# Turning q and k on TensorE instead of VectorE for the first batch's strided heads and the second batch's local heads

## The chip, the cores and the metric

The kernel runs on one core of a Trainium2 chip. The metric is the device time in microseconds of one execution, as the median of three runs. Where an engine is named: PE is TensorE, DVE is VectorE, ACT is ScalarE, POOL is GpSimd, SP is SyncE (here it only issues DMAs).

## The reference

Four batches of eight heads, 576 positions, head size 64. The first four heads of a batch attend locally, the other four with a stride; the attention's output goes through two MLPs.

```
scores = scale * np.matmul(q, k.transpose(0, 1, 3, 2))
mask_local = (rel >= 0) & (rel < stride)                      # heads 0 to 3, stride 32
mask_strided = (rel >= 0) & (pos[None, :] % stride == pos[:, None] % stride)   # heads 4 to 7
attn = softmax(where(mask, scores, -1e9));  x = attn @ v      # x becomes 2304 x 512
y = (x @ w_a) * (x @ w_b) @ w_out                             # d_ff 1536
h = y @ w_in;  out = (h * sigmoid(h)) @ w_out2                # d_ff 2048
```

## The kernel before, in words

The order of the work is written out by hand: each engine runs its instructions in the order in which the Python code issues them, and waits where a value or a buffer is not ready.

**Start-up.** The attention of batch 0 is cut into nine units: five of local heads (128 queries each) and four of strided heads. A loop over stages `s` from -1 to 16 runs one step of each unit per stage, in the order of the letters in `ORDER`: within a stage come V (`values`), then Q (the strided q and k of batch 0 are turned, by the table `TQ`, in stages 2, 3 and 4), then S (`scores`, L414 and L417), T (`turn`, L500) and K. K is `keep_warm` (L773): matmuls of constants whose result nobody reads, so many per stage as `WARM1` says. The DMAs of the start-up are issued in the order of `LOADS[-2]`: small letters on SP's queue, capitals on ACT's; `t` is one step of the loads of batch 0's strided q and k, `u` one of batch 1's local q and k, `s` and `v` are values, `w` weights as 64-bit words.

The local q and k of batch 0 are turned on TensorE in pairs of positions (`turn_pair`, L296, evacuated at L307 and L309). All other q and k are loaded by `load_qk` (L264): eight DMAs, each of 32-element pieces (128 bytes) into 32 partitions, laid out so that four VectorE stream transposes (`transpose_qk`, L275, 128x576 each) make `qT` and `kT`.

**Blocks.** After the start-up the MLP of the first tokens runs in blocks `p`: kinds a, b (up, L683, 12 matmuls of 512 columns) and o (down, L1345, 12). The first four up blocks have half of their matmuls in the start-up (`PART`, four times 6); the last two of these halves come after the last unit of batch 0, and the other halves are blocks 0 to 3, 6 matmuls each. Block 4 is the first o block; it needs the gated product of block 1 (L1331 on VectorE, then a split: L693 on ScalarE, L694 on VectorE). The attention of batches 1 to 3 is woven into these blocks by `plan_attention`: `PLAN[1]` gives the blocks at which the nine units of batch 1 are prepared, a unit's scores stand two blocks later, its turn five and its values six. At the head of a block come the functions planned under "load", "tensor" and "turned", then the block's matmuls, then the planned VectorE and ScalarE work.

**Buffers.** In batch 0 `att_tile` hands out seven PSUM banks in turn (later four); for batches 1 to 3 it hands out two, so the third request waits for the readers of the first. The tiles `qld` and `kld` have one buffer each.

Around block 0 VectorE and ScalarE also finish two weight tiles that were begun early (`merge_w`, L642 to L655; their splits L675 and L676).

Of the kernel before, what the change touches and what calls it, by code (L numbers as in the profile page):

```python
# [9 lines left out]
F32 = mybir.dt.float32  # L10
# [8 lines left out]
P = 128  # L19
# [14 lines left out]

PREP = {-1: (0, 1, 2, 3, 4), 3: (5, 6), 5: (7,), 7: (8,)}
PAIR = {-1: 0, 0: 1, 2: 2}
TQ = {2: (0,), 3: (1,), 4: (2, 3)}

LOADS = {
    -2: (  # L40
        "q0 Q1 i M1 K2 S1 w0 V1 k0 k1 s1 t4 t5 v0 M7 r8 s1 s1 s1 w2 s2 s1 S1 w1 s1 s1 s1 w4 "
        "w3 s4 Q2 u2 u5 u2"
    ),
    -1: "b",
    8: "w5 w6",
# [48 lines left out]


PLAN = {
# [3 lines left out]
}  # L100
# [11 lines left out]
def attention_gated_mlp_silu_mlp(  # L112
# [15 lines left out]
    nc = tc.nc  # L128
    B, H, S, D = q.shape
# [32 lines left out]
    lpool = att_ctx.enter_context(tc.tile_pool(name="lpool", bufs=1, side="right"))  # L162
    qpool = att_ctx.enter_context(tc.tile_pool(name="qpool", bufs=2, side="right"))
    apool = att_ctx.enter_context(tc.tile_pool(name="apool", bufs=3, side="right"))

    ident = cpool.tile([P, P], F32, name="ident")
# [11 lines left out]
    def acc_tile(i):  # L178
        return accp.tile([P, 512], F32, tag=f"acc{i}", name=f"acc{i}")

    def ring_tile():
        return ringp.tile([P, 512], F32, tag="ring", name="ring")

    att_turn = [0]
    feed = [nc.sync]

    def att_tile(wide):
        n = att_turn[0]
        att_turn[0] += 1
        if wide:  # L190
            n %= wide
            if n < 2:
                return ring_tile()
            if n >= 4:
                return acc_tile(n - 4)
        return attp.tile([P, 512], F32, tag="att", name="att")
# [36 lines left out]
    class Batch:  # L233
# [38 lines left out]
        def transpose_qk(self, ty, one=None):  # L272
            for i in range(4) if one is None else (one,):
                t, o, c = self.loaded[i // 2], self.T[ty][i // 2], i % 2
                nc.vector.transpose(out=o[:, c], in_=t[:, c].rearrange("p j i -> p (j i)"))  # L275

        def load_pair(self, m, i):

            if not self.T:
                self.T[0] = [qpool.tile([P, 2, S], F32, tag=nm, name=nm) for nm in ("qT", "kT")]  # L280
                self.pairs = {}
            p0, n = PAIRS[m]
            self.pairs[m, i] = t = rpool.tile([P, 4, 2 * D], F32, tag="raw", name="pair")
            feed[0].dma_start(
                out=t[:n],
                in_=(q, k)[i][self.b, 0:4, 2 * p0:2 * (p0 + n), :].rearrange("h (p s) d -> p h (s d)", s=2),
            )
# [392 lines left out]
    def up(ps, w, x, T, chunks=range(CC)):  # L680
        for c in chunks:
            for wi, xi in PASSES:
                nc.tensor.matmul(  # L683
                    ps[:, :T],
                    lhsT=w[:, wi, c * P:(c + 1) * P],
                    rhs=x[:, xi, c, :T],
                    start=(c == 0 and wi == 0 and xi == 0),
                    stop=(c == CC - 1 and wi == 1),
                )
# [12 lines left out]
    def plan_attention(batch, s0, first, end):  # L702

        add = lambda at, place, f, *a: plan.setdefault((at, place), []).append((f, a))

        def spread(loads, n, s0, s1):
            for m in range(n):
                add(s0 + m * (s1 - s0) // n, "load", next, loads, None)

        turn1 = first[NL - 1] + 2  # L710
        for one in range(4):
            add(s0 + one // 2, "prepare", batch.transpose_qk, 0, one)
            add(turn1 - 4 + one, "prepare", batch.transpose_qk, 1, one)
        spread(batch.load_qk(1), 9, s0 + 2, turn1 - 7)
        spread(batch.load_vs(), 4 * TAKE + 5, s0 + 4 * (batch.b > 1), first[NL] + 3)
        for u, s in enumerate(first):
            add(s, "prepare", batch.prepare, u)
            add(s + 2, "tensor", batch.scores, u)
            add(s + 2, "mask", batch.mask, u)
            add(s + 2, "mask", batch.largest, u)  # L720
            add(s + 2, "softmax", batch.softmax, u)
            add(s + 2, "normalise", batch.guard, u)
            add(s + 2, "normalise", batch.normalise, u)
            add(s + 5, "tensor", batch.turn, u)
            add(s + 5, "turned", batch.turned, u)
            add(s + 6, "tensor", batch.values, u)
            add(s + 6, "store", batch.store, u)
        after = Batch(batch.b + 1, False)
        if after.b < B:
            spread(after.load_qk(0), 9, turn1 + 2, end)  # L730
            spread(after.load_vl(), 10, first[NL] + 7, end)
        return after
# [30 lines left out]
    with tc.manual_schedule():  # L763
# [6 lines left out]
        def keep_warm(n):  # L770

            for _ in range(n):
                nc.tensor.matmul(idle, lhsT=still, rhs=nc.const_aps.tensor(1.0, [P, 512], BF16), start=True, stop=True)  # L773

        batch = Batch(0, 7)
        nu = len(batch.units)
        every = lambda loads: [None for _ in loads]
        after = Batch(1, False)
        qs0, vs0, q1 = batch.load_qk(1), batch.load_vs(), after.load_qk(0)
        vl0 = batch.load_vl()  # L780

        masks = [epool.tile(list(t.shape), F32, tag="e", name="mask") for t in (mask_loc, mask_str)]
# [32 lines left out]
        for s in range(-1, max(nu + LV, max(PART), max(CONV) + 1) + 1):  # L815
            def stage(f, d):
                if 0 <= s - d < nu:
                    f(s - d)

            if s >= TAIL:  # L820
                batch.wide = 4
            now, last = CONV.get(s), CONV.get(s - 1)
            for step in ORDER:
                if step == "P" and s in PAIR:
                    for i in range(2):
                        batch.turn_pair(PAIR[s], i)
                        batch.turned_pair(PAIR[s], i)
                elif step in "SVTXLGNOU":
                    f, d = {
                        "S": (batch.scores, 0), "L": (batch.largest, 0), "X": (batch.softmax, 1),  # L830
                        "G": (batch.guard, 1), "N": (batch.normalise, 1), "T": (batch.turn, LT),
                        "U": (batch.turned, LT), "V": (batch.values, LV), "O": (batch.store, LV),
                    }[step]
                    stage(f, d)
                elif step == "K":
                    keep_warm(WARM1.get(s, 0))
                elif step == "A" and s in PART:
                    i = PART[s]
                    partial[i] = acc_tile(i)
                    up(partial[i], split[i], x_tile(0), G, (0, 1))  # L840
                elif step == "Q":
                    for i in TQ.get(s, ()):
                        batch.transpose_qk(1, i)
                elif step == "R":
                    for u in PREP.get(s, ()):
                        batch.prepare(u)
                elif step in "012" and now is not None:
                    merge_w(now, int(step), True)
                elif step == "B" and now is not None:
                    rebase_w(now, True)  # L850
                elif step == "Y" and last is not None and last < EARLY:
                    keep_w(last)
                    split_w(last)
                elif step == "W":
                    startup_loads(LOADS.get(s, ""))
        batch = after
# [356 lines left out]
        for m, key in enumerate(in_order):  # L1213
            t = ready[key]
            if m >= 4:
                t = max(t, held[in_order[m - 4]][1])
# [5 lines left out]
        for m, key in enumerate(in_order):  # L1222
            t = used[key][0] - LEAD_SPLIT
            t = max(t, used[in_order[m - 5]][1] if m >= 5 else (m - 5) * BLOCK)
# [34 lines left out]
        for key in in_order:  # L1259
            t = splits[key]  # L1260
# [3 lines left out]
            elif key[0] == "B":  # L1264
                n, c = key[1:]
                kind, j = ("ab"[c], n[1]) if n[0] == "o" else ("i", n[1] + c)
                needs((kind, j), (n, c, 0), t)
            elif key[0] == "B22":
                for c in range(2):
                    n = key[1]  # L1270
                    kind, j = ("ab"[c], n[1] + H1) if n[0] == "o" else ("i", n[1] + c + H2)
                    needs((kind, j), (n, c, 1), t)
            elif key[0] == "T12":
                n, c = key[1:]
# [21 lines left out]
        for m, key in enumerate(in_order):  # L1296
            lo, _, piece = need[key]
            t = lo - LEAD_RAW
            t = max(t, need[in_order[m - 10]][1] + 0.01 if m >= 10 else (m - 10) * BLOCK)
# [3 lines left out]
        p = 0  # L1303
        ys = {}
        for ph, g in PHASES:
# [7 lines left out]
            for kind, j in half[ph]:  # L1313
                if batch.b < B and p == PLAN[batch.b][0]:
                    batch = plan_attention(batch, *PLAN[batch.b])
                work = block(p)
                w = next(work)
                if kind in "abi":
                    rest = range(CC)
                    if p in partial:  # L1320
                        ps, rest = partial[p], (2, 3)
                    else:
                        ps = ring_tile()
# [9 lines left out]
                    else:  # L1333
# [4 lines left out]
                            out=g2, in0=th, scalar=1.0, in1=ps, op0=ALU.add, op1=ALU.mult  # L1338
                        )
                        acts[j] = split_act(g2, T)  # L1340
                elif kind == "o":
                    h = acts.pop(j)
# [9 lines left out]
                    if j == N1 - 1:  # L1352
                        ys[g] = y = xpool.tile([P, 2, CC, G], F32R, tag="x%d" % HOMES["y"][g], name="y")
                        for d in range(CC):
                            nc.scalar.copy(out=y[:, 0, d], in_=accs[d])
                            nc.vector.tensor_tensor(
                                out=y[:, 1, d], in0=accs[d], in1=y[:, 0, d].bitcast(F32), op=ALU.subtract
# [3 lines left out]
                else:  # L1361
                    h = acts.pop(j)
# [14 lines left out]
            for t in range(T // P):  # L1377
                pool, tag = ((epool, "e"), (epool, "e"), (tpool, "a"), (tpool, "h32"))[t]
# [48 lines left out]
```

## Time and profile before

| | us |
|---|---|
| median of 3 runs (956.31 to 957.92) | 957.8 |
| the profiled execution | 954.39 |
| its span, first to last instruction | 952.6 |
| TensorE busy in the span | 928.5 (97%) |
| VectorE busy | 663.9 (70%) |
| ScalarE busy | 542.6 (57%) |
| mean granted TensorE clock | 0.988 |

Times in the trace are microseconds from the first instruction of the span. A busy share is an average over stages with different limits. The ends of matmuls are modelled, so that a TensorE shown as busy can still be slower than its peak. The granted clock is a share of 2.4 GHz; in this trace it is 1.00 or 0.50 (1.2 GHz).

### The profile page before, as it was taken

The numbers are of one execution on the slowest core, as the hardware profiler recorded it, in microseconds if no ns is written. First come the engines' busy times: TensorE is split into PE (matmuls) and PEld (weight loads), VectorE is DVE, ScalarE is ACT, GpSimd is POOL, SyncE is SP. The second block draws the span as 40 slices with busy tenths as digits, with TensorE's granted clock in tenths as the row PEclk, the third lists the DMA queues.
The fourth block names the chain that finished last, engine by engine and source line by source line (L and its number), as shares of the span: only waits on it lengthen the run. The fifth ranks groups of instructions, "written<-read, shape, count | busy, mean of one in ns | idle before, by whom it ended". The sixth has DMA issues, their size and how long they took to land.

```text
span 952.6 us, 15861 instructions
## 1 busy us (share of the span) xinstructions
PE 928.5 (97%) x5626; PEld 749.6 (79%) x5626; DVE 663.9 (70%) x1248; ACT 542.6 (57%) x1274; POOL 80.4 (8%) x138
## 2 busy tenths in 40 slices
PE   9999999999999899999999999999999989999998
PEld 5767777787777677778888888888998768888897
DVE  4588888866767766666777666765587666765475
ACT  3558788566667665465544444345565555554364
POOL 2232222111111110100000000000000000000000
PEclk9799999999999999999999999999999999999999
DMA  9999899898698994322332222223464121234371
GB/s 165 198 271 269 248 254 271 248 294 240 224 267 208 264 223 133 105 86 89 100 105 83 67 67 67 57 83 112 126 185 125 44 67 56 78 107 148 108 212 47
DMA packets 163647, 145.29 MB, mean 153 GB/s; under 512 B 96800, under 2 KB 119904, under 8 KB 163568
## 3 DMA queue, kind: packets, MB, share of 16 engines
q1 hardware_dynamic: 154758, 121.81, 48.1%
q0 software_dynamic: 6720, 21.63, 6.8%
q10 hardware_dynamic: 2090, 0.84, 0.5%
q8 instruction: 44, 0.72, 0.3%
q14 instruction: 35, 0.29, 0.1%
HBM read 121.70 MB, written 22.54 MB: 151 GB/s over the span
## 4 chain that ended last, share of the span: by engine, by line
PE 75%; DVE 11%; ACT 8%; issue 3%; DMA 2%; SPq 0%; DVEq 0%; POOL 0%; ACTq 0%; POOLq 0%
PE ring L683 17%; PE ring L958 10%; PE att L958 8%; PE acc L1019 8%; PE acc L1365 7%; PE acc L1145 4%; PE att L1019 4%; PE ring L1019 4%; PE acc L1345 4%; PE acc L683 3%; ACT prs L466 2%; DVE w L676 2%; DVE raw L650 2%; PE att L540 1%; ACT raw L647 1%
## 5 line engine op out<-in xcount | busy, mean ns | idle before, releaser
L683 PE MATMUL ring<-x,w 128*128 128x512 f32 (+1 forms) x816 | 165.5, 356 | 1.5 <-DVE w L676 1.5
L683 PEld LDWEIGHTS ring<-x,w 128*128 128x128 f32 x816 | 132.4, 189 | 23.4 <-DVE w L676 2.0
L1241 DVE TENSOR_TENSOR w<-raw,w 128x512 fp32r<-128x512 f32 (+1 forms) x164 | 106.3, 656 | 30.3 <-ACT w L1240 27.5
L1240 ACT CAST w<-raw 128x512 fp32r<-128x512 f32 (+1 forms) x164 | 95.8, 593 | 18.6 <-PE att L1019 11.0
L676 DVE TENSOR_TENSOR w<-raw,w 128x512 fp32r<-128x512 f32 x136 | 92.8, 686 | 8.6 <-ACT w L675 7.9
L683 PE MATMUL ring<-y,w 128*128 128x512 f32 x384 | 96.1, 400 | 2.2 <-DVE g L1337 0.8
L1365 PE MATMUL acc<-w,h 128*128 128x512 f32 x384 | 93.9, 394 | 0.0
L683 PEld LDWEIGHTS ring<-y,w 128*128 128x128 f32 x384 | 71.9, 191 | 18.8 <-DVE w L676 1.1
L675 ACT CAST w<-raw 128x512 fp32r<-128x512 f32 x136 | 82.8, 619 | 4.0 <-DVE raw L655 3.9
L1365 PEld LDWEIGHTS acc<-w,h 128*128 128x128 f32 x384 | 70.9, 188 | 15.4
L693 ACT CAST h<-h 128x512 fp32r<-128x512 f32 (+1 forms) x48 | 27.3, 568 | 95.1 <-DVE h L1331 48.1
L1345 PE MATMUL acc<-h,w 128*128 128x512 f32 x288 | 70.8, 395 | 0.0
L958 PE MATMUL ring<-operands,w 128*128 128x512 f32 x240 | 61.4, 398 | 2.4 <-ACT w L1240 2.0
L694 DVE TENSOR_TENSOR h<-g,h 128x512 fp32r<-128x512 f32 (+1 forms) x64 | 39.9, 624 | 33.4 <-ACT h L693 33.2
L1345 PEld LDWEIGHTS acc<-h,w 128*128 128x128 f32 x288 | 53.0, 188 | 11.5
L693 ACT CAST h<-g 128x512 fp32r<-128x512 f32 (+1 forms) x64 | 36.3, 568 | 44.8 <-DVE g L1337 30.4
L958 PE MATMUL att<-operands,w 128*128 128x512 f32 x240 | 60.2, 395 | 0.0
L958 PE MATMUL ring<-x,w 128*128 128x512 f32 x240 | 59.2, 391 | 1.0 <-ACT u L969 1.0
L466 ACT ACTIVATE prs<-sm,nm 128x54 f32<-128x54 f32 (+1 forms) x120 | 39.8, 336 | 30.5 <-DVE nm L452 30.4
L958 PEld LDWEIGHTS ring<-operands,w 128*128 128x128 f32 x240 | 44.7, 188 | 14.8 <-ACT w L1240 2.7
L650 DVE SCALAR_TENSOR_TENSOR raw<-words,raw 128x512 int32<-128x512 int32 x68 | 47.6, 699 | 9.5 <-ACT raw L647 8.9
L958 PEld LDWEIGHTS ring<-x,w 128*128 128x128 f32 x240 | 44.9, 188 | 11.1 <-ACT u L969 1.4
(200 smaller groups left out, 1577.1 us busy)
## 6 DMA issues: line engine op xcount, KB each, us to landing
raw<-keptp SPq DMA_DIRECT2D x80, 256.0 KB
raw<-kepti SPq DMA_DIRECT2D x64, 256.0 KB
words<-in_moe_w_out_dram SPq DMA_DIRECT2D x28, 512.0 KB
raw<-kepto SPq DMA_DIRECT2D x48, 256.0 KB
raw<-kepta SPq DMA_DIRECT2D x36, 256.0 KB
raw<-keptb SPq DMA_DIRECT2D x36, 256.0 KB
words<-in_moe_w_in_dram SPq DMA_DIRECT2D x16, 512.0 KB
words<-in_moe_w_a_dram SPq DMA_DIRECT2D x12, 512.0 KB
```

The source lines that it names most:

```text
L466: nc.scalar.activation(out=place[s], in_=src[:, s], func=AF.Exp, bias=st["nm"][:, s:s + 1], scale=1.0, accum_out=su[:, s:s + 1],)
L650: nc.vector.scalar_tensor_tensor(out=z, in0=high, scalar=SIGN, in1=z, op0=ALU.bitwise_and, op1=ALU.bitwise_or)
L675: nc.scalar.copy(out=o[:, 0], in_=t)
L676: nc.vector.tensor_tensor(out=o[:, 1], in0=t, in1=o[:, 0].bitcast(F32), op=ALU.subtract)
L683: nc.tensor.matmul(ps[:, :T], lhsT=w[:, wi, c * P:(c + 1) * P], rhs=x[:, xi, c, :T], start=(c == 0 and wi == 0 and xi == 0), stop=(c == CC ...
L693: nc.scalar.copy(out=o[:, 0, :T], in_=t32[:, :T])
L958: nc.tensor.matmul(self.acc[acc], lhsT=w[:, wi, (2 * part + c) * P:(2 * part + c + 1) * P], rhs=x[:, xi, c], start=(begin and c == 0 and m ...
L1019: nc.tensor.matmul(accs[d], lhsT=lhsT, rhs=rhs, start=(first and wi == 0 and xi == 0), stop=(last and wi == 1))
L1240: nc.scalar.copy(out=o[:, 0, cols], in_=t)
L1241: nc.vector.tensor_tensor(out=o[:, 1, cols], in0=t, in1=o[:, 0, cols].bitcast(F32), op=ALU.subtract)
L1345: nc.tensor.matmul(accs[d], lhsT=w[:, wi, d * P:(d + 1) * P], rhs=h[:, xi], start=(j == 0 and wi == 0 and xi == 0), stop=(j == N1 - 1 and ...
L1365: nc.tensor.matmul(accs[t][:, :DM], lhsT=h[:, xi, t * P:(t + 1) * P], rhs=w[:, wi, :], start=(j == 0 and wi == 0 and xi == 0), stop=(j == ...
```

## The change

For batch 0's strided heads and batch 1's local heads, `load_rows` takes the place of `load_qk`: twelve DMAs in place of eight, of whole rows of 64 elements (256 bytes). Positions 0 to 511 go by head, one DMA each for q and k (128 partitions, four positions each, 512 rows); the last 64 positions go by two heads (64 partitions, 128 rows). `turn_rows` transposes them on TensorE into a PSUM bank: i = 0 to 3 stands for q or k and one pair of heads (four transposes of 128x128), i = 4 and 5 for the last 64 positions of q and of k (two transposes of 64x128). `turned_rows` copies the bank to `qT` or `kT`: i = 0 and 3 on ScalarE, the others on VectorE. In the start-up, i = 0 stands in stage 2, 1 and 4 in stage 3, and 2, 3 and 5 in stage 4. For batch 1, i = 0 and 2 stand at the head of block 0, 4 and 5 at block 1, 1 and 3 at block 2, with two PSUM banks to share; the first scores move from block 3 to block 4, and all nine units of batch 1 one block later. Batch 1's strided q and k, and all of batches 2 and 3, are loaded and turned as before.

```
-TQ = {2: (0,), 3: (1,), 4: (2, 3)}
+TQ = {2: (0,), 3: (1, 4), 4: (2, 3, 5)}
+TOKENS = 4
+ROWS_A = (0, 3)
-        "q0 Q1 i M1 K2 S1 w0 V1 k0 k1 s1 t4 t5 v0 M7 r8 s1 s1 s1 w2 s2 s1 S1 w1 s1 s1 s1 w4 "
-        "w3 s4 Q2 u2 u5 u2"
+        "q0 Q1 i M1 K2 S1 w0 V1 k0 k1 s1 t6 t7 v0 M7 r8 s1 s1 s1 w2 s2 s1 S1 w1 s1 s1 s1 w4 "
+        "w3 s4 Q2 u4 u5 u4"
-    1: (0, [1, 2, 7, 8, 13, 18, 19, 24, 25], 35),
+    1: (0, [2, 3, 8, 9, 14, 19, 20, 25, 26], 35),
+        def load_rows(self, ty):
+            tiles = [lpool.tile([P, TOKENS + 1, 4, D], F32, tag=nm, name=nm) for nm in ("qld", "kld")]
...
+            whole = P * TOKENS
+            for src, t in zip((q, k), tiles):
+                for h in range(4):
+                    hp, c = divmod(h, 2)
+                    feed[0].dma_start(
+                        out=t[:, :TOKENS, 2 * c + hp],
+                        in_=src[self.b, 4 * ty + h, :whole].rearrange("(n p) d -> p n d", p=P),
+                    )
+                    yield
+                for hp in range(2):
+                    h0 = 4 * ty + 2 * hp
+                    feed[0].dma_start(
+                        out=t[:S - whole, TOKENS, hp::2],
+                        in_=src[self.b, h0:h0 + 2, whole:].rearrange("c p d -> p c d"),
+                    )
+                    yield
+        def turn_rows(self, i):
...
+            self.turns[i] = ps = att_tile(self.wide)
+            if i < 4:
+                parts = [(self.loaded[i // 2][:, n, 2 * (i % 2):2 * (i % 2) + 2], P) for n in range(TOKENS)]
+            else:
+                n = S - P * TOKENS
+                parts = [(self.loaded[i - 4][:n, TOKENS, 2 * c:2 * c + 2], n) for c in range(2)]
+            for m, (t, n) in enumerate(parts):
+                nc.tensor.transpose(ps[:, m * n:(m + 1) * n], t.rearrange("p h d -> p (h d)"), ident[:n, :n])
+        def turned_rows(self, ty, i):
+            ps, o = self.turns.pop(i), self.T[ty][i // 2 if i < 4 else i - 4]
+            copy = nc.scalar.copy if i in ROWS_A else nc.vector.tensor_copy
...
         for one in range(4):
-            add(s0 + one // 2, "prepare", batch.transpose_qk, 0, one)
+            if batch.b > 1:
+                add(s0 + one // 2, "prepare", batch.transpose_qk, 0, one)
             add(turn1 - 4 + one, "prepare", batch.transpose_qk, 1, one)
-        spread(batch.load_qk(1), 9, s0 + 2, turn1 - 7)
+        for m, i in enumerate((0, 2, 4, 5, 1, 3) if batch.b == 1 else ()):
+            add(s0 + m // 2, "tensor", batch.turn_rows, i)
+            add(s0 + m // 2, "turned", batch.turned_rows, 0, i)
+        spread(batch.load_qk(1), 9, s0 + 2 + (batch.b == 1), turn1 - 7)
-        qs0, vs0, q1 = batch.load_qk(1), batch.load_vs(), after.load_qk(0)
+        qs0, vs0, q1 = batch.load_rows(1), batch.load_vs(), after.load_rows(0)
                     for i in TQ.get(s, ()):
-                        batch.transpose_qk(1, i)
+                        batch.turn_rows(i)
+                        batch.turned_rows(1, i)
```

## Rows read from the trace of the kernel before

**Rows 1.** The page, busy time of each engine: us, share, instructions.

```profile
PE 928.5 (97%) x5626; PEld 749.6 (79%) x5626; DVE 663.9 (70%) x1248; ACT 542.6 (57%) x1274; POOL 80.4 (8%) x138
```

**Rows 2.** The chain that ended last, in order of time: start, us, what.

```profile
9.23 1.06 PE att L296 x8
...
16.71 0.51 PE acc L296 x12
...
20.93 0.37 PE att L500 x2
...
31.24 1.25 PE att L417 x12
...
35.91 1.46 PE acc L417 x12
...
47.73 1.40 PE acc L683 x6
```

**Rows 3.** Waits of VectorE, 0 to 110 us: total us, times, longest.

```profile
DVE nm L452 <- PE ring L417: 4.7, 4, 2.4
```

**Rows 4.** Waits of TensorE, 0 to 160 us: total us, times, longest.

```profile
PE att L429 <- DVE kT L275: 2.2, 2, 1.8
PE att L429 <- DVE x L571: 1.1, 2, 0.9
```

**Rows 5.** Stretches: length, busy us (PE, PEld, DVE, ACT, POOL), granted clock, DMA.

```profile
33.00:46.60 13.60, 13.60 (x105) 9.33 (x103) 7.67 (x25) 7.74 (x41) 2.71 (x3) 0.50 1.16 187
...
61.20:63.60 2.40, 0.30 (x2) 0.13 (x2) 2.40 (x5) 0.00 (x0) 0.00 (x0) 1.00 1.05 240
63.70:67.10 3.40, 3.40 (x36) 2.62 (x36) 2.58 (x7) 2.87 (x8) 0.00 (x0) 0.50 1.02 375
```

**Rows 6.** Timeline of TensorE around blocks 0 to 4: start, us, instructions.

```profile
53.65 7.50 PE L683 MATMUL acc<-x,w 128*128 128x512 f32 x30
62.98 0.30 PE L429 MATMUL att<-kT,qT 64*32 64x64 f32 x2 [1.83 <-DVE kT L275]
63.64 1.10 PE L429 MATMUL att<-kT,qT 64*32 64x64 f32 x30 [0.36 <-DVE kT L275]
64.67 2.76 PE L683 MATMUL acc<-x,w 128*128 128x512 f32 x6
67.36 0.70 PE L429 MATMUL att<-kT,qT 64*32 64x64 f32 x32
67.99 3.04 PE L1345 MATMUL acc<-h,w 128*128 128x512 f32 x12
```

**Rows 7.** Timeline of VectorE around the end of the start-up.

```profile
46.08 0.29 DVE L571 TENSOR_TENSOR x<-att,x 128x128 fp32r<-128x128 f32 x1
...
53.14 0.56 DVE L571 TENSOR_TENSOR x<-att,x 128x288 fp32r<-128x288 f32 x2 [0.21 <-PE acc L773]
...
59.40 1.52 DVE L676 TENSOR_TENSOR w<-raw,w 128x512 fp32r<-128x512 f32 x2
60.83 1.43 DVE L275 STREAM_TRANSPOSE qT<-qld 128x576 f32<-128x576 f32 x2
62.19 1.40 DVE L275 STREAM_TRANSPOSE kT<-kld 128x576 f32<-128x576 f32 x2
```

**Rows 8.** Timeline of ScalarE around the end of the start-up.

```profile
59.57 0.62 ACT L675 CAST w<-raw 128x512 fp32r<-128x512 f32 x1 [1.29 <-DVE raw L655]
```

**Rows 9.** Timeline of all engines in the start-up (SPq: SP issues a DMA).

```profile
8.11 5.60 SPq L264 DMA_DIRECT2D qld<-in_q_dram  x4
8.37 0.68 DVE L309 TENSOR_SCALAR qT<-ring 64x512 f32<-64x512 f32 x1 [4.57 <-PE ring L296]
...
17.84 0.78 DVE L275 STREAM_TRANSPOSE qT<-qld 128x576 f32<-128x576 f32 x1 [0.16 <-DMA qld<-in_q_dram]
...
18.28 1.41 SPq L321 DMA_DIRECT2D vl<-in_v_dram  x2
...
19.74 6.04 SPq L330 DMA_DIRECT2D vl<-in_v_dram  x8
```

More of the change, by code (lines that the diff above doesn't have):

```diff
@@ L275, in transpose_qk @@
                 nc.vector.transpose(out=o[:, c], in_=t[:, c].rearrange("p j i -> p (j i)"))
+        def load_rows(self, ty):
+            tiles = [lpool.tile([P, TOKENS + 1, 4, D], F32, tag=nm, name=nm) for nm in ("qld", "kld")]
+            self.loaded = tiles
+            self.T[ty] = [qpool.tile([P, 2, S], F32, tag=nm, name=nm) for nm in ("qT", "kT")]
+            whole = P * TOKENS
[15 more added lines that the diff above has]
+        def turn_rows(self, i):
+            self.turns = getattr(self, "turns", {})
+            self.turns[i] = ps = att_tile(self.wide)
[9 more added lines that the diff above has]
+            copy = nc.scalar.copy if i in ROWS_A else nc.vector.tensor_copy
+            if i < 4:
+                copy(out=o[:, i % 2, :P * TOKENS], in_=ps)
+            else:
+                n = S - P * TOKENS
+                copy(out=o[:, :, P * TOKENS:], in_=ps[:, :2 * n].rearrange("p (c t) -> p c t", c=2))
         def load_pair(self, m, i):
```

## The prediction, made before the changed kernel ran

> **What bounds the kernel now.** I read the page first: TensorE is busy 97% of the span, VectorE 70%, ScalarE 57% [rows 1]. So the question for every edit is whether it gives TensorE more to do in a stretch where TensorE sets the pace, or takes away one of its few waits.
>
> The chain in order of time, read second, shows which engine sets the pace in the start-up. From 9.2 us to block 0 it runs on TensorE alone, one piece ending where the next begins; the rows shown are samples of it [rows 2]. The waits say the same from the other side: VectorE waits for TensorE, 4.7 us for one kind of score alone [rows 3], while the largest wait of TensorE before 160 us is 2.2 us, for the VectorE transposes of batch 1 at block 3 [rows 4]. The warm-up matmuls explain it: they fill what would be gaps, and they stay. The reader is to see that in the start-up a faster VectorE brings nothing, and that each new TensorE instruction moves everything behind it.
>
> The stretches, read third, show two half-clock pieces that matter here: TensorE's granted clock is 0.50 (1.2 GHz) from 33.0 to 46.6 us in the start-up, and again from 63.7 to 67.1 us, just behind a stretch of 2.4 us in which TensorE is busy 0.3 us and VectorE all the time [rows 5]. I call that second place the join: the start-up's last VectorE work (two early weight tiles, 59.40 to 60.9) stands in front of the four stream transposes (60.83 to 63.6) [rows 7], and TensorE, done with blocks 0 to 2 at about 61, cannot begin the first scores before 62.98 [rows 6].
>
> **The change in the start-up.** Added on TensorE: four runs of four full transposes and four small ones. The nearest rows: eight transposes with a 128-column identity and 64 columns of weights take 1.06 us, 0.13 each; two of exactly the new shape take 0.37, 0.185 each with the handover to the next kind; twelve of 48 columns take 0.51, 0.043 each [rows 2]. A run of four I put at 0.55 (between 4 x 0.13 and 4 x 0.185), a small one at 0.075 (between 0.043 and 0.13): 4 x 0.55 + 4 x 0.075 = 2.5 us; ends 16 x 0.13 + 4 x 0.043 = 2.25 and 16 x 0.185 + 4 x 0.13 = 3.5. All of it is on the path: +2.5.
>
> Taken from VectorE: four stream transposes, about 0.75 each (0.78 alone, 1.43 and 1.40 for two [rows 7, 9]), 3.0 in all. Put there: two copies of 512 columns at 0.68 (an evacuation of that length [rows 9]) and two of 128 columns at 0.3 (0.29 [rows 7]), 2.0; on ScalarE two copies, 1.4 by the same row. I cost these at nothing because both engines run behind TensorE here; if that cover were gone, VectorE's side would give 1.0 back and ScalarE's cost 1.4.
>
> The loads: eight DMAs were issued from 8.11 to 18.28, with some waits between. Eight of the new ones have 512 rows each; the nearest is the load of v, eight of up to 576 rows in 6.04 us, 0.75 each; the four small ones I put at 0.7 (two in 1.41) [rows 9]: 8 x 0.75 + 4 x 0.7 = 8.8 us in place of 10.2. The last q load before was issued by 13.71 and VectorE saw it at 17.84, 4.1 us later [rows 9]; the new q loads are out by 8.1 + 4 x 0.75 + 2 x 0.7 = 12.5, so there by 16.6, and the first transposes stand at about 17.2. No wait, with 0.6 us to spare; at worst TensorE waits about 1 us. Batch 1's loads, once issued from 36 to 44 us, come a little earlier too; they wait for the same two buffers, which TensorE has read by about 27. What stands behind them on SP's queue (values, weights, two stores) comes 1 to 3 us earlier and is waited for by nobody: cost nothing, gain nothing.
>
> **The change at the join.** I follow TensorE from 53.65, in times of the trace before, and add the 2.5 at the end, since VectorE's last work that needs the start-up's scores, at 53.14, already waited 0.21 us for TensorE [rows 7] and moves with it. Six matmuls of 512 columns take 1.40 [rows 2].
>
> - Two last halves from the start-up, 2.80: 56.45. Transposes i = 0 and 2, 1.1: 57.55. Block 0's six: 58.95.
> - Transposes i = 4 need the PSUM bank of i = 0, i = 5 that of i = 2 (two banks). The copy of i = 0 stands on ScalarE behind the split that ends at 59.57 + 0.62 = 60.19 [rows 8]: free at 60.87. The copy of i = 2 stands on VectorE behind the two weight splits that end at 60.92 [rows 7]: free at 61.60. So the wait of before is not removed; it moves from the first scores to the small transposes, 61.60 - 58.95 = 2.65 us, less 0.15 in which i = 4 runs. Queued behind it on TensorE is all of block 1. i = 5 ends at 61.75.
> - Block 1's six: 63.15. Transposes i = 1 and 3: 64.25. Blocks 2 and 3: 67.05. Their banks are free by then: the copies of i = 4 and 5 need 0.3 each, those of i = 1 and 3 have both blocks to run under.
> - Unit 0's scores, 0.63 to 0.70 [rows 6]: 67.7, and block 4 begins. Its gated product (block 1's evacuation from 63.2, then 0.7 and 0.6 us on each engine) is ready at about 65.3. Behind block 4 come unit 1's scores, 0.63, which before stood ahead of it. So compare 68.3 with 67.99 [rows 6]: +0.3 us.
>
> In this balance 2.5 us of transposes and a new wait are paid by the end of the old wait (2.2 and the drain before it) and of the half clock behind it, where six matmuls took 67.36 - 64.67 = 2.69 in place of 1.40 and unit 0's scores 1.03 in place of 0.63, 1.7 in all [rows 6]. I add 0.3 for restarts: the rows have 30 matmuls from 53.65 to 60.98, 7.33 us, where 5 x 1.40 is 7.0.
>
> Later blocks: batch 1's units stand one block later, so the same waits meet other kinds of blocks. TensorE waits 1.1 us for `x` there [rows 4]; I take no change, with 1 us either way.
>
> **Sum.** 2.5 + 0.3 + 0.3 = 3.1 us, 952.6 to 955.7 us of span. The profiled execution took 954.39, 1.8 beyond its span and 3.4 below the median of 957.8; against the median the forecast is **960.9 us**.
>
> **A rule that speaks against the change.** Transposes stand in the start-up already, at a granted clock of 1.00 (two at 20.93 [rows 2], outside the half-clock stretches of [rows 5]). The Trainium skill, page "TensorE: Matmul & The Clock Gate", Part 4 (PE-mode transpose), says that transposes do not count as busy time for the clock as matmuls do, and puts one of 128x128 bf16 at about 275 ns in a kernel. With that figure, as an estimate from that page, 16 would cost 4.4 us; the spacing of the rows decides for 2.1 to 3.0. No row here shows as many in so short a time as the change has, so what the rule would do to the clock is rival 2.
>
> **The rivals.**
>
> 1. The clock falls at the join again. A TensorE stretch nearly empty for 2.4 us stood ahead of the fall before [rows 5]; the new wait is as long, though broken by two transposes and followed at once by matmuls. Price 1.7 us, as above: 962.6.
> 2. The clock falls around the new transposes of stages 2 to 4. For it: ten of the twenty stand in one stage with few long matmuls. Against it: seven warm-up matmuls just ahead. One more half-clock stretch costs 1.7 (the join's) to 3.8 (rival 4's): 962.6 to 964.7. That is what the rule cited above would lead to.
> 3. The new wait does not come, because ScalarE and VectorE reach their copies of i = 0 and 2 earlier. For it: VectorE's order is only partly tied to TensorE. Against it: the two splits ahead of those copies end at 60.19 and 60.92. It saves 2.6: 958.3, no measurable change.
> 4. The start-up's half-clock stretch goes or shrinks, since the work meets the clock at another moment. Of 13.6 us, work of the kind whose 1.25 became 1.46 [rows 2] would give back 2.0, matmuls whose 1.40 became 2.69 6.5; I take 3.8: 957.1, no measurable change. Nothing in the change adds work between 33 and 46 us, which speaks against it.
> 5. Faster: VectorE's backlog, not TensorE, sets the time of the join. Then the start-up's transposes are free, VectorE arrives 1.0 us earlier, and passes the join with 0.68 + 0.6 in place of 2.8, another 1.5; the low clock behind it (1.7) goes as well: 957.8 - 4.2 = 953.6. For it: VectorE is busy without a break through the 2.4 us stretch [rows 5]. It decides if VectorE's store at 53.14 no longer waits for TensorE; before, it did wait [rows 7].
>
> **Chances.** My forecast 0.32, rival 1 0.24, rival 2 0.08, rival 3 0.14, rival 4 0.10, rival 5 0.12. About 0.2%, 1.9 us, is what a measurement of this kernel can tell from no change. Slower by more: forecast and rivals 1 and 2, 0.64, less a little for a forecast that comes out low: 0.62. Within it: rivals 3 and 4 and that little: 0.25. Faster: rival 5 and a little: 0.13. The range leaves out rival 5 and the upper part of rival 2: 956.6 to 964.3. It covers the forecast with its bounds, 2.25 to 3.5 in the start-up, as much at the join, and 1 us in later blocks. The likeliest case by itself is 959.4 to 962.5.
>
> **What would show each step right or wrong.** Right: block 0's first matmul some 2.5 us after 53.65; no VectorE transposes before block 12; TensorE waiting at the transposes of block 1 for copies on ScalarE and VectorE, with no wait at the first scores; the granted clock at 1.00 behind it; then all blocks about 3 us late to the end. Wrong: block 0 no later than before (rival 5), no wait at block 1 (rival 3), another half-clock stretch (rivals 1 and 2), or the long one shorter (rival 4). Most of all the forecast falls if the start-up has slack on TensorE that the chain does not show, or if batch 1's units, one block later, change the waits behind 68 us by more than 1 us.

## The result, and the profile after

| | before | changed |
|---|---|---|
| median of 16 executions, us | 956.16 | 961.37 |
| lowest and highest | 951.14, 959.75 | 956.17, 973.77 |
| profiled execution, its span | 954.39, 952.6 | 958.96, 957.1 |
| mean granted clock in the profile | 0.988 | 0.996 |

The changed kernel is slower: ratio 1.0063, 95% interval 1.0038 to 1.0089, which is 6.0 us (3.6 to 8.5) of 956. The forecast of 960.9 and its range hold it. The ratio leaves out executions over 1.5% above the fastest of their kernel; the table has them. The changed kernel's executions fall into two groups: five at 968.6 to 973.8 with a mean granted clock of 0.976 to 0.984, eleven at 956.2 to 964.8 with 0.989 to 0.998. The kernel before has no such upper group.

The page of the changed kernel has the busy shares of [rows 1] to within a point:

```profile
PE 926.6 (97%) x5659; PEld 750.8 (78%) x5666; DVE 662.4 (69%) x1248; ACT 544.0 (57%) x1278; POOL 81.2 (8%) x138
```

The timeline of TensorE (lines have moved: L313 is the new transpose, L461 and L464 the start-up's scores, L476 batch 1's, L730 an up matmul, L1397 a down matmul):

```profile
13.83 0.27 PE L461 MATMUL ring<-mask_loc,ident_b 128*64 128x256 bf16 x1 [1.47 <-issue]
...
18.76 0.66 PE L313 MATMUL ring<-ident,qld 128*128 128x128 f32 x4
...
21.38 0.86 PE L313 MATMUL att<-ident,qld 128*128 128x128 f32 x6
...
25.56 0.60 PE L313 MATMUL acc<-ident,kld 128*128 128x128 f32 x4
26.00 0.86 PE L313 MATMUL ring<-ident,kld 128*128 128x128 f32 x6
...
28.93 0.30 PE L461 MATMUL acc<-mask_str,ident_b 128*64 128x324 bf16 x1
...
49.76 1.62 PE L730 MATMUL acc<-x,w 128*128 128x512 f32 x6 [2.33 <-DVE x L618]
...
55.89 3.02 PE L730 MATMUL acc<-x,w 128*128 128x512 f32 x12
58.75 0.60 PE L313 MATMUL att<-ident,qld 128*128 128x128 f32 x4
59.18 0.60 PE L313 MATMUL att<-ident,kld 128*128 128x128 f32 x4
59.54 1.64 PE L730 MATMUL acc<-x,w 128*128 128x512 f32 x6
62.37 0.34 PE L313 MATMUL att<-ident,qld 64*128 64x64 f32 x2 [1.19 <-ACT qT L319]
63.26 0.30 PE L313 MATMUL att<-ident,kld 64*128 64x64 f32 x2 [0.55 <-PE att L313]
...
68.73 0.70 PE L476 MATMUL att<-kT,qT 64*32 64x64 f32 x32
69.36 3.01 PE L1397 MATMUL acc<-h,w 128*128 128x512 f32 x12
72.36 0.87 PE L476 MATMUL att<-kT,qT 64*32 64x64 f32 x32
```

Read from the bottom, the join looks as forecast: there is no wait at the first scores any more (2.2 us in [rows 4]) and 1.19 + 0.55 us of waiting at the small transposes instead. From the last halves at 55.89 to block 4 at 69.36 it is 13.47 us. With 0.87 for unit 1's scores, which now stand behind block 4, that makes 14.34, as much as from 53.65 to 67.99 in [rows 6]. In the start-up the rows show two things that I had not forecast. The first scores start at 13.83 us, behind 1.47 us of idle time; before, they started at 12.20 without a gap. And the first up matmuls wait 2.33 us for VectorE's store of `x`. This execution has no half-clock stretch in the start-up, where the profile of before had 13.6 us of it [rows 5]; that hides in the profile what the start-up lost.

The late scores can be followed on ScalarE. First the kernel before, then the changed one (ACTq is ScalarE's queue issuing a DMA):

```profile
9.62 0.32 ACTq L284 DMA_DIRECT2D pair<-in_q_dram  x1
9.97 1.28 ACT L307 ACT_TABLE_LOAD   x1 [9.97 <-DMA pair<-in_k_dram]
11.27 0.62 ACT L307 ACTIVATE qT<-ring 64x512 f32<-64x512 f32 x1
```

```profile
11.48 0.32 ACTq L331 DMA_DIRECT2D pair<-in_q_dram  x1
11.83 1.28 ACT L354 ACT_TABLE_LOAD   x1 [11.83 <-DMA vl<-in_v_dram]
13.12 0.61 ACT L354 ACTIVATE qT<-ring 64x512 f32<-64x512 f32 x1
```

ScalarE's evacuations stand behind the issue of the third q piece (`Q2`). That issue now waits for a later load of v and comes 1.9 us later. By the program's instruction list the first scores wait for the first of these evacuations: it ends at 13.73, and they start at 13.83. The lists of the two programs also say why the issue is late: in them a DMA waits for the earlier DMA that counts its landing on the same counter, and the third q piece's counter is now that of the first `vl` load on ScalarE's queue, which was issued at 6.37 us.

```
before   L284 DMA pair<-in_q_dram 48x4x128 [waits DMAHW7_49,DMAHW0_49,PE_49]
changed  L368 DMA vl<-in_v_dram 64x4x64 [waits DMAHW2_49]
changed  L331 DMA pair<-in_q_dram 48x4x128 [waits DMAHW2_49,DMAHW0_49,PE_49]
```

### The profile page after: what moved, and what is told of

The parts are those of the page before. It is cut to its first block, busy times and chain, and to the rows that moved or that the text cites. A ratio compares the mean times of both kernels' runs of the same rounds, so it can differ in the third digit from the quotient of the medians.

```text
span 957.1 us, 15959 instructions
## 1 busy us (share of the span) xinstructions
PE 926.6 (97%) x5659; PEld 750.8 (78%) x5666; DVE 662.4 (69%) x1248; ACT 544.0 (57%) x1278; POOL 81.2 (8%) x138
## 4 chain that ended last, share of the span: by engine, by line
PE 75%; DVE 12%; ACT 7%; issue 3%; DMA 2%; ACTq 0%; POOL 0%; DVEq 0%; SPq 0%; POOLq 0%
PE ring L730 17%; PE ring L1010 10%; PE att L1010 8%; PE acc L1071 8%; PE acc L1417 7%; PE acc L1197 4%; PE att L1071 4%; PE ring L1071 4%; PE acc L1397 4%; PE acc L730 3%; ACT prs L513 2%; DVE raw L697 2%; DVE w L723 2%; PE att L587 1%; DVE raw L702 1%
## 5 line engine op out<-in xcount | busy, mean ns | idle before, releaser
L730 PE MATMUL ring<-x,w 128*128 128x512 f32 (+1 forms) x816 | 165.0, 356 | 1.5 <-DVE w L723 1.5
L730 PEld LDWEIGHTS ring<-x,w 128*128 128x128 f32 x816 | 132.5, 189 | 23.2 <-DVE w L723 2.0
L730 PE MATMUL ring<-y,w 128*128 128x512 f32 x384 | 95.6, 398 | 2.2 <-DVE g L1389 0.8
L730 PEld LDWEIGHTS ring<-y,w 128*128 128x128 f32 x384 | 71.5, 190 | 18.6 <-DVE w L723 1.1
L1397 PE MATMUL acc<-h,w 128*128 128x512 f32 x288 | 71.1, 397 | 0.0
L1397 PEld LDWEIGHTS acc<-h,w 128*128 128x128 f32 x288 | 52.8, 188 | 11.7 <-ACT prs L513 0.2
L1010 PEld LDWEIGHTS att<-operands,w 128*128 128x128 f32 x240 | 45.7, 190 | 11.2
```

Source lines behind the costliest of these rows:

```text
L730: nc.tensor.matmul(ps[:, :T], lhsT=w[:, wi, c * P:(c + 1) * P], rhs=x[:, xi, c, :T], start=(c == 0 and wi == 0 and xi == 0), stop=(c == CC ...
L1010: nc.tensor.matmul(self.acc[acc], lhsT=w[:, wi, (2 * part + c) * P:(2 * part + c + 1) * P], rhs=x[:, xi, c], start=(begin and c == 0 and m ...
L1397: nc.tensor.matmul(accs[d], lhsT=w[:, wi, d * P:(d + 1) * P], rhs=h[:, xi], start=(j == 0 and wi == 0 and xi == 0), stop=(j == N1 - 1 and ...
```

## The experiments

The theory at this point: the loss is the start-up's, made of the transposes' own time, the late third q piece, and the half clock that follows its idle gap. The rivals: the transposes themselves let the clock fall; batch 1's later units make the loss; the shifted PSUM banks make it. Each run has 6 to 12 executions beside 27 to 31 of the kernel before, whose median is 956.43 us beside x0 to x3, 956.52 beside x5 to x9 and 955.68 beside x10 to x13. The line at 965.5 us lies between the two groups of each kernel that has two.

| run | median, us | ratio to before | interval | executions over 965.5 us |
|---|---|---|---|---|
| x0, the change again | 968.09 | 1.0089 | 1.0054 to 1.0124 | 6 of 10 |
| x1, batch 0 alone | 964.56 | 1.0090 | 1.0058 to 1.0123 | 3 of 6 |
| x2, batch 1 alone | 954.96 | 0.9979 | 0.9962 to 0.9995 | 0 of 12 |
| x3, later units alone | 953.51 | 0.9983 | 0.9965 to 1.0000 | 0 of 12 |
| x5, idle transposes | 956.70 | 1.0008 | 0.9991 to 1.0025 | 0 of 12 |
| x7, third q piece first | 958.81 | 1.0022 | 1.0004 to 1.0041 | 0 of 12 |
| x8, gap filled | 962.02 | 1.0060 | 1.0038 to 1.0082 | 0 of 8 |
| x9, four more DMAs | 956.79 | 1.0019 | 1.0000 to 1.0038 | 0 of 12 |
| x10, one bank left out | 961.58 | 1.0069 | 1.0037 to 1.0101 | 5 of 12 |
| x11, q piece and bank | 958.45 | 1.0015 | 0.9996 to 1.0034 | 0 of 12 |
| x12, batch 1 with four banks | 951.30 | 0.9935 | 0.9913 to 0.9957 | 0 of 6 |
| x13, all three mends | 955.24 | 0.9977 | 0.9959 to 0.9995 | 0 of 12 |

**x1: batch 0's rows alone.**

```
-        "w3 s4 Q2 u4 u5 u4"
+        "w3 s4 Q2 u2 u5 u2"
-    1: (0, [2, 3, 8, 9, 14, 19, 20, 25, 26], 35),
+    1: (0, [1, 2, 7, 8, 13, 18, 19, 24, 25], 35),
-        ... after.load_rows(0)
+        ... after.load_qk(0)
```

(and batch 1's turns on VectorE as before)

> Only batch 0's strided q and k come in rows and are turned on TensorE; batch 1 is as before. If the twenty transposes are simply added to a TensorE that sets the pace, block 0's first matmul comes about 2.5 us later than before and the time is 2 to 4 us (0.2% to 0.4%) longer. If the loss is made by the row loads holding back other loads, the first scores start about 1.6 us later than the 12.20 us of before, as in the changed kernel. If the transposes let the clock fall, a half-clock stretch begins before 33 us. If VectorE sets the pace of the start-up, no change or 1 us faster.

Slower by 0.9%, more than the transposes' time can be. The first scores start at 13.47 us. Its waits of TensorE, 10 to 70 us, show the start-up's two new waits and the old one of the join:

```profile
PE acc L730 <- DVE x L618: 2.3, 1, 2.3
PE att L476 <- DVE kT L278: 2.0, 2, 1.6
PE ring L461 <- issue: 1.5, 1, 1.5
```

So batch 0's part carries the whole loss; three of the six executions are in the upper group.

**x2: batch 1's rows alone.** `TQ`, batch 0's loads and its VectorE transposes as before, the rest as changed.

> Only batch 1's local q and k come in rows and are turned on TensorE, and its units begin a block later; batch 0 is as before. By the prediction: TensorE waits about 2.6 us less at the first scores and about as long at the small transposes of block 1; 0 to 2 us longer in all. If the start-up alone makes the loss: no change or 1 us faster. If batch 1's later units make it, 2 to 3 us longer, with waits behind 68 us.

Faster by 0.2% (0.5 to 3.6 us), the first scores at 12.13 us. Batch 1's part is a small gain, where I had put the join at +0.3. The gain is not to be seen at the join of its trace: TensorE waits 0.59, 1.60 and 0.56 us at the transposes, and the clock falls behind them:

```profile
60.60:64.00 3.40, 3.40 (x14) 2.91 (x13) 1.98 (x3) 1.20 (x2) 0.00 (x0) 0.50 1.07 330
```

From the last halves (50.49) to block 4 (66.74), with unit 1's scores, it is 17.12 us, against 14.34 before.

**x3: the later units alone.** The kernel before with the changed `PLAN[1]`.

> The kernel before with batch 1's units one block later and nothing else. The transposes on VectorE then have one block more (1.4 us) before the first scores, so the wait of 2.2 us there falls to about 1 us: if later blocks are neutral, 1 to 2 us faster. If the shifted units meet worse blocks, as the changed kernel's trace suggests (1.1 us more of waits between 68 and 170 us), no change.

1.6 us faster at an interval that touches zero; the wait at the join falls from 2.2 to 0.6 us, and block 4 then waits 0.7 us for its product. Later units are not the loss. They are also all that x2's gain needs: x3 gains about as much with the transposes left on VectorE, so x2 does not show that moving them to TensorE gained anything.

**x0: the change again.** No edit.

> The changed kernel again, for its spread. 4 to 6 us longer than before. If its loss is fixed work, the trace has block 0 about 2 us late and batch 1's units 3 us late by 170 us whatever the clock does. If the loss is the clock's, the granted clock differs from run to run and the time with it, about 8 us for each 0.01 of mean clock.

Six of ten executions are in the upper group. The profile caught one of them; stretches with the granted clock in the column behind the five busy times:

```profile
12.00:14.90 2.90, 1.63 (x34) 1.28 (x36) 0.03 (x1) 2.46 (x5) 0.00 (x0) 1.00 0.91 179
15.00:31.90 16.90, 16.54 (x140) 10.56 (x141) 5.31 (x22) 6.31 (x35) 1.38 (x3) 0.50 0.77 180
```

and its TensorE:

```profile
13.19 0.27 PE L461 MATMUL ring<-mask_loc,ident_b 128*64 128x256 bf16 x1 [1.53 <-issue]
...
20.56 1.12 PE L313 MATMUL ring<-ident,qld 128*128 128x128 f32 x4
```

TensorE is idle for 1.5 us ahead of 13.19, busy 1.63 of 2.90 us, and the clock falls just behind, for 17 us of the start-up. The first new transpose comes at 20.56, 5.6 us after the fall: it cannot have caused it.

**x5: transposes without the change.**

```
                     for i in TQ.get(s, ()):
                         batch.transpose_qk(1, i)
+                    for _ in range({2: 4, 3: 6, 4: 10}.get(s, 0)):
+                        nc.tensor.transpose(idle[:, :P], ident, ident)
```

> The kernel before, with twenty transposes of a constant added on TensorE at the places of the change (4, 6 and 10 in stages 2, 3 and 4); loads and VectorE's transposes are as before, and nobody reads the added results. If the added TensorE work alone is what the start-up pays, 2 to 3 us longer, the first scores at 12.2 us as before, and no half-clock stretch before 30 us. If transposes let the clock fall, several runs lie 5 to 12 us above before with a mean clock under 0.985. If the loss is made by the loads, 2 us longer at most.

0.8 us longer (0.9 shorter to 2.4 longer), no execution in the upper group. From the first scores to the first strided ones its trace takes 15.03 us, against 12.70 before and 15.10 in the changed kernel (28.93 - 13.83): the stretch grows by 2.3 to 2.4 us, about the 2.5 that I had put on it, but how much of that reaches the end lies between nothing and all.

**x7: the third q piece on SP's queue ahead of the rows.**

```
-        "... k0 k1 s1 t6 t7 v0 ... w3 s4 Q2 u4 u5 u4"
+        "... k0 k1 s1 q2 t6 t7 v0 ... w3 s4 u4 u5 u4"
```

> The changed kernel with the third q piece of batch 0's local heads loaded on SP's queue ahead of the row loads, in place of ACT's queue behind them. If the wait on ACT's queue is the main loss, the first scores are back at about 12.2 us, no half-clock stretch begins before 30 us, and the time is 0 to 3 us above before. If the transposes are the loss, 5 us and more remain, with low mean clocks in some runs.

The first scores start at 11.63 us with no gap ahead of them, and nothing lies above 961.9:

```profile
11.16 0.55 PE L343 MATMUL ring<-ident,pair 112*64 112x112 f32 x4
11.63 0.30 PE L461 MATMUL ring<-mask_loc,ident_b 128*64 128x256 bf16 x1
```

With 0.22% left of 0.63 to 0.89%, the wait on ScalarE's queue, with the half clock that follows it, is by the middle values two thirds to three quarters of the loss. The edit takes away a little more than the change had added: the first scores are 0.6 us earlier than the 12.20 of before.

**x8: the gap filled.** The changed kernel with `WARM1` at nine in place of two matmuls in stage -1.

> The changed kernel with nine in place of two warm-up matmuls at the end of stage -1, 1.5 us that fill TensorE's wait ahead of the first scores. If that idle time is what lets the clock fall, the first scores stay at about 13.5 us but no run has a half-clock stretch from 15 us, and the time falls to 2 to 4 us above before. If the transposes let the clock fall, the low runs stay: 5 to 12 us above before.

The first scores are as late as before the mend (13.54). No execution is over the line of 965.5, though the two highest, 965.34 and 965.37, lie just under it. The median stays: 962.02. So the idle gap, not the lateness, opens the way to the upper group. I was wrong that the mend would bring the time to within 4 us of before: without the gap the ratio is 1.0060, as in the change, so the early half clock makes the upper group, and what is left of the loss has other causes: the late start, the transposes, the wait of the up matmuls. How it is shared out is open; x8's own trace has other half-clock stretches in the start-up (3.4 us from 31.8 and 10.2 from 42.0).

**x9: four more small DMAs in the kernel before.**

```
-        "... k0 k1 s1 t4 t5 v0 ..."
+        "... k0 k1 s1 t4 t5 e4 v0 ..."     # e: ident[:, 16m:16m+16] into a tile of its own
```

> The kernel before with four more small DMAs on SP's queue behind the loads of batch 0's strided q and k (constants into tiles that nobody reads), as many as the change adds there; nothing else. If the change's four additional DMAs shift which earlier DMA the third q piece on ACT's queue has to wait for, the first scores come at 13.2 to 13.8 us in place of 12.2, TensorE idles 1.5 us ahead of them, and some runs have a half-clock stretch from about 15 us: 4 to 9 us longer in the mean. If only the row loads' traffic or the transposes matter, the first scores stay at 12.2 and the time is unchanged.

The first scores stay at 11.92 us and the third q piece still waits for the counter `DMAHW7`. My idea that the number of DMAs alone shifts the counter fell. The instruction lists show what did shift it: the loads of SP and ACT take eight counters in turn, in the order of the list. The third q piece is the sixteenth load there in the kernel before and in x9, whose four DMAs come behind it, and the nineteenth in the changed kernel, where three of the new row loads of q stand ahead of it. Why the list puts them ahead stays open; that the wait costs is shown by x7.

**x10: one bank left out of the rotation, and x11: that and the q piece first.**

```
                         batch.turned_rows(1, i)
+                    att_turn[0] += s == 4
```

> The changed kernel with one PSUM bank of the rotation of seven left out behind the transposes of stage 4, so that six new requests become seven and every later tile of batch 0 is in the bank of before. If the shift of the rotation makes the wait of 2.3 us of the first up matmuls (their bank still holds values that VectorE has to store), that wait is gone and the time is 1 to 3 us under the changed kernel's; the late first scores and the low runs stay. If that wait is only VectorE's backlog, it stays at about 2 us.

> The changed kernel with both: the third q piece on SP's queue ahead of the row loads, and one bank left out. If the wait on ACT's queue, the shifted rotation and the transposes' own time are all of the start-up's loss, the time is 2 us under the kernel with the q piece alone (958.8), at about that of before (within 1.5 us), with no half-clock stretch before 25 us. If something else is in it, it stays 2 us and more above before.

In both the wait of the first up matmuls for VectorE is gone; all waits of TensorE in x11, 10 to 70 us:

```profile
PE att L313 <- ACT qT L319: 1.2, 1, 1.2
PE att L313 <- PE att L313: 0.6, 1, 0.6
```

Six requests in a rotation of seven banks had put the first up matmuls onto a bank with values that VectorE still had to store; a seventh puts things back. But the time does not follow: x10 is where the change is, x11 (1.0015) where x7 is (1.0022). The mechanism is right, and its price was not measurable. The trace of x11 shows what the join costs when the clock falls there. It has the waits of the change, a half-clock stretch of 3.4 us right behind them, and from the last halves (52.80) to block 4 (67.87), with unit 1's scores, 15.94 us in place of 14.34:

```profile
61.20:64.60 3.40, 3.40 (x14) 2.90 (x13) 1.15 (x2) 0.81 (x2) 0.00 (x0) 0.50 1.10 361
```

**x12: x2 with four banks for batch 1's turns, and x13: the change with all three mends.**

```
-            self.turns[i] = ps = att_tile(self.wide)
+            self.turns[i] = ps = att_tile(4 if self.b == 1 else self.wide)
```

> Batch 0 as before, batch 1's local q and k in rows as in the change, with four PSUM banks in place of two for its six turns. If the wait of the small transposes in block 1 comes from the two banks, it shrinks from 2.2 us to about 1 us (then at block 2), and the time is 2 to 3 us under before. If VectorE's backlog holds the join whatever the banks do, the wait comes back at the first scores and the time is that of batch 1 alone in rows, 2 us under before.

> The whole change with all three: third q piece first, one bank left out, four banks for batch 1's turns. If each wait is its own, about 1 us under the run with the first two; 0 to 2 us under before. If the start-up's added transposes still cost their 2 us, within 1 us of before.

x12 is 6.2 us faster than before (4.1 to 8.3) by the ratio, 4.4 by the medians, in six executions, and the best kernel of this study. Its TensorE at the join:

```profile
50.06 3.02 PE L730 MATMUL acc<-x,w 128*128 128x512 f32 x12
52.92 0.60 PE L313 MATMUL att<-ident,qld 128*128 128x128 f32 x4
53.35 0.60 PE L313 MATMUL ring<-ident,kld 128*128 128x128 f32 x4
53.71 1.71 PE L730 MATMUL acc<-x,w 128*128 128x512 f32 x6
55.34 0.33 PE L313 MATMUL ring<-ident,qld 64*128 64x64 f32 x2
55.52 0.28 PE L313 MATMUL att<-ident,kld 64*128 64x64 f32 x2
55.73 1.66 PE L730 MATMUL acc<-x,w 128*128 128x512 f32 x6
57.71 0.66 PE L313 MATMUL att<-ident,qld 128*128 128x128 f32 x4 [0.31 <-ACT qT L319]
58.60 0.63 PE L313 MATMUL ring<-ident,kld 128*128 128x128 f32 x4 [0.23 <-PE att L313]
...
62.52 3.01 PE L1396 MATMUL acc<-h,w 128*128 128x512 f32 x12
```

From the last halves to block 4 it is 12.46 us, where the change took 13.47; the waits at the turns are 0.54 in place of 1.74, and the clock is 1.00. That is 3.8 us less than in the trace of x2, which differs in the banks alone, and the ratios of the two are 0.0044 (4.2 us) apart. x13 against x11 is the same step: in x13 TensorE does not wait at the join at all, nothing falls to half clock there, its join (51.24 to 62.66) is 3.65 us shorter, and its median is 3.2 us lower. By these traces what four banks take away is the wait and the half clock that can follow it. Against the kernel before, x12's join is only 1.0 us shorter; where the rest of its gain lies is not shown. The half clock of the start-up may be part of it: 3.4 us in x12's trace and 13.6 in the one of before.

x13, with the start-up's turns on TensorE as well, is 2.2 us faster than before (0.5 to 3.9) by the ratio, 0.4 by the medians, and 4 us behind x12: batch 0's part does not pay even when mended.

## Why the prediction was right, and where its steps were not

**Sign and size.** Forecast +3.1 us (960.9), measured +6.0 (3.6 to 8.5) by the ratio, +5.2 by the medians. That 960.9 lies so near to 961.37 is luck: the forecast stood on 957.8 for the kernel before, 1.6 over the 956.16 of sixteen executions. The eleven executions of the lower group have a mean of 959.7, 3.5 over the mean of before (956.2); the five others lie some 11 us higher still. So the size fits the case that the forecast described, and the half clock that it had left to a rival came in three to six of ten executions. But the fit is in part made of two errors. By x1 and x2 batch 0's part costs 8.6 us where the sum had 2.5, and batch 1's gains 2.0 where the sum had a loss of 0.6 (0.3 for the join and 0.3 for restarts).

**"All of it is on the path: +2.5."** As a stretch of TensorE's time, right: 2.4 us more from the first to the strided scores. As a share of the end, unsettled (x5: -0.9 to 2.4). I had read the chain of before as TensorE's alone up to block 0; it passes to VectorE at 53.14 us, 3.3 us earlier. In x5's trace TensorE waits 0.67 us for VectorE's store in block 0, so that not all that is added ahead of it need arrive.

**"What stands behind them ... cost nothing, gain nothing."** This step failed. I looked at SP's queue and at when rows land, and found rightly that no transpose waits for its rows. I did not look at ScalarE's queue: there the third q piece came to wait for a load of v, 1.9 us, and ScalarE's evacuations and the first scores with it. x7 shows the price: 0.41 to 0.67%, 4 to 6 us by the middle values, together with the half clock.

**Banks of the rotation.** I did not count that six more requests shift every later tile of batch 0. It made a wait of 2.3 us and no measurable loss.

**"The wait of before is not removed; it moves."** Right in place and cause: it stood at block 1's turns, on ScalarE's copy of i = 0 and VectorE's of i = 2, and four banks took most of it away (x12). Its size was 1.74 us where I had 2.5: VectorE's splits ended 6.67 us after the start of the last halves (62.56 less 55.89), where before they ended 7.27 after it. In x2, where the start-up is that of before, it was 2.75. That batch 1's part as a whole gains 2 us, x2, I had not forecast. The join of x2's trace does not hold this gain, and x3 has about as much without any transposes moved; where it comes from stays open.

**Later blocks.** Put at nothing, give or take 1 us, and right within that. From block 4 to 120 down matmuls later the changed kernel needs 103.37 us where the kernel before needs 101.90; 0.87 of the difference is unit 1's scores, counted with the join above, and 0.6 is left. TensorE waits longer for `ptl` on ScalarE, over 0 to 165 us, first in the kernel before, then in the changed one:

```profile
PE att L540 <- ACT ptl L512: 0.7, 1, 0.7
PE att L587 <- ACT ptl L559: 2.9, 3, 1.3
```

By the middle value of x3 the later units all the same gain more at the join than they lose there.

**Rivals.** Rival 2 was real in its place, wrong in its cause and too low in its price. The upper group is 19 of the 44 executions of the four kernels that have the unfilled gap (change, x0, x1, x10) and none of the 98 of the other nine. Two traces lie in that group, those of x0 and x10, and in both the clock falls at 14 to 15 us, ahead of the new transposes; that it fell there in the other seventeen is inferred from their times. Twenty idle transposes opened no upper group (x5). The price was 1.7 to 3.8 us; the upper group lies 11 us over the lower one. The Trainium skill, page "TensorE: Matmul & The Clock Gate", Part 4 (PE-mode transpose), has transposes not counting as busy time for the clock in the way that matmuls do. No run here shows that: x5's mean clock over its executions is 0.992, that of the kernel before beside it 0.990.

Rival 4 came in the profile of the change, whose start-up has no half-clock stretch at all; the length of that stretch differs from execution to execution (13.6 us in the profile of before, 17.1 in those of x3 and x9, 3.4 in x2's). Rival 1 did not come in the profile of the change, whose clock is 1.00 from 4 to 335 us, but it did in those of x2, x10 and x11: 3.4 us of half clock behind the new wait, and in x11 a price of 1.6 us, where I had put 1.7. Rival 3 fell: the new wait is there (1.19 and 0.55 us). Rival 5 fell: batch 0's part gives nothing back (x1).

## What to carry to other kernels

When a change adds DMAs, look at every DMA queue for what now waits behind what, ScalarE's above all, since its compute stands behind its issues: here one issue, 1.9 us late, moved the first scores by 1.6 us and cost, with the half clock behind its gap, most of the loss by the middle values (x7). Count what a change takes from a rotation of buffers, and give a burst of requests as many buffers as it has before the first is read: two more banks turned a gain of 0.2% into 0.65% (x2, x12), and the same step is worth 3.2 us between x11 and x13. And move work from a waiting engine to the busiest one only where that engine waits: batch 1's transposes stood in a wait of TensorE and did not cost, batch 0's did not pay even when mended. Whether moving batch 1's transposes gained anything is a different question: later units alone (x3) gained about as much as x2, so try the plan by itself first.

## What the runs showed of the hardware that I had not expected

An idle gap of 1.5 us on TensorE near the start was followed in two of the four traces that have it by a fall of the granted clock to 0.50, within 2 us of the gap's end (x0 and x10; not in the change and x1). It held for 17.1 and 20.5 us of nearly unbroken but short TensorE work (16.54 of 16.90 us busy in x0). In the kernels that have this gap the spread is wide: the change took 956 to 974 us.

The waits around the small transposes of the join, 1.7 to 2.2 us in all, were followed by 3.4 us at 0.50 in the traces of x2, x10 and x11. In those of the change, x0, x7 and x8, with waits of 1.7 us too, the clock stayed at 1.00.
